# Attention scores in two halves of keys, a 352-byte pad at the upper end of SBUF, and a new work order

## The chip, the core and the metric

The kernel runs on one core of a Trainium2 chip. Its engines work side by side: TensorE (PE) multiplies matrices from SBUF into PSUM, VectorE (DVE) and ScalarE (ACT) work element by element and are the ones that read PSUM here, GpSimd (POOL) works on SBUF, and SyncE (SP) issues the DMA transfers used here. PSUM has 8 banks of 512 float32 columns on 128 partitions. The metric is the device time of one execution, in microseconds; lower is better.

## The reference

All in float32. B = 4, H = 8 heads, S = 576 positions, D = 64, so a row of the mixer has 512 channels.

```python
q_rot, k_rot = (rotate(q), rotate(k))
scores = scale * np.matmul(q_rot, k_rot.transpose(0, 1, 3, 2))
scores = scores - np.max(scores, axis=-1, keepdims=True)
attn = np.exp(scores)
attn = attn / (np.sum(attn, axis=-1, keepdims=True) + 1e-09)
x = np.matmul(attn, v)              # then the heads of a position side by side
xt = x.transpose(0, 2, 1)
h = np.maximum(xt @ w_tok1, 0.0) @ w_tok2      # 576 -> 256 -> 576
u = x + h.transpose(0, 2, 1)
h2 = np.maximum(u @ w_ch1, 0.0) @ w_ch2        # 512 -> 1536 -> 512
return u + h2
```

## The kernel before

**Stages.** First the attention, with the token mixer of batch 0 in it; then the token mixers of batches 1 to 3; then the channel mixer. Most products are made from float32r halves: each operand is split into a high and a low part, and three matmuls (high by high, high by low, low by high) add up in one PSUM bank.

**Attention.** 16 pairs of heads, one after the other in a software pipeline. For a pair, `prep` loads k, q and v, rotates k and q on GpSimd (VectorE for the first pair), transposes them on TensorE (L372) and splits them (L386 on ScalarE, L389 on VectorE). `pair` then goes through five steps, `ORDER = [0, 1, None, 2, 3]`: four row tiles of 128 queries for both heads, and `None`, the last 64 queries of both heads in one tile. Of each step:

- `qk` (L474; L444 for `None`): scores of 128 queries against 576 keys in two halves of `W2 = 288` keys, three passes each. The two heads of L474 sit in two row tiles of the array (mode "row"); L444 uses the whole array (mode "full"). Each score tile takes two neighbouring PSUM banks, one per half, asked for by `Buf(banks, True)`, so a row tile holds four banks. One PE task makes all.
- `mx` (L426, VectorE): one instruction over 128 x 576 scores in PSUM multiplies by -1/8, writes the product to `p` in SBUF and accumulates the minimum into `nm`.
- `ex` (L430, ScalarE): exponential in place in `p`, with `nm` as bias, and the sum of the row.
- `tr` (L494; L455): transposes of `p` on TensorE, two banks; `cp` (L499; L460, L464) copies them to `pt`, on ScalarE or VectorE, whichever the planner thinks will be done first.
- `pv` (L512): 20 matmuls in column tiles after steps 1 and 3 add up the output, copied to `oT` by `p1` (L515); at the end of a pair L541 transposes it and L546, L550 divide by the row sums.

**Order.** Every step is a task with an engine, an assumed duration, dependencies, buffers and a priority. `Plan.run` is a list scheduler that runs while the program is built: it takes, for each engine, the tasks that can start within `SLACK` of the earliest one, and of these the one with the lowest priority value. Priorities are 9 for a pair plus a number from the table `AT`. A change of TensorE's mode is charged `SWITCH = 0.15` us. Banks are handed out singly or as neighbouring pairs (`Banks.pick`). The token weights (`tok_weights`, `f64_split`: L581 to L602, eight instructions a block on ScalarE, VectorE and GpSimd) are tasks of the same plan with high values in `AT["tok"]`, mostly behind the attention's.

**Mixers.** The token mixer (L682, L704) and the channel mixer (L799 up, L822 down) run matmuls of 128 x 128 weights by 512 columns. The channel mixer goes through the 1536 hidden channels in four groups of 384. In each group five chunks of rows (4, 4, 4, 4 and 2 tiles of 128) pass L799 (36 matmuls a chunk, over 512 columns, 256 for the last) and L822 (9 matmuls over 512 columns a tile). L799 multiplies the weights `c1h`, `c1l` with the activations `uh`, `ul`; L822 multiplies `gh`, `gl` (the hidden layer) with the weights `c2h`, `c2l`. Weight set 0 serves groups 1 and 3, set 1 groups 2 and 4.

**Placement in SBUF.** Pools are allocated from the lower end, or, with `side="right"`, from the upper end. Set 0 and all `uh`, `ul` are in the lower pool `wc`; set 1 and all `gh`, `gl` are in the upper pool `late`, which takes the place of the token weights' upper pool `wt`. Each of these tiles has a size that is a multiple of 512 bytes a partition. In the program before, the lower ones start 128 bytes past a multiple of 512, the upper ones 480 bytes past.

Of the kernel before, what the change touches and what calls it, by code (L numbers as in the profile page):

```python
# [9 lines left out]
F32 = mybir.dt.float32  # L10
F32R = mybir.dt.float32r
U32 = mybir.dt.uint32
ACTF = mybir.ActivationFunctionType
# [175 lines left out]

AT = {'load': [372.85, 448.93, 617.75], 'rot': [1101.38, 721.17], 'pt': [672.28, 599.15], 'bd': [281.77], 'qk': [647.35, 345.47, 341.63, 278.21, 427.4], 'mx': [288.84, 281.93, 421.34, 414.86, 343.1, 594.04, 868.63, 796.12, 321.94, 410.88], 'ex': [324.09, 378.12, 428.41, 1197.56, 379.36, 390.42, 467.2, 298.25, 872.52, 998.23], 'tr': [413.54, 441.31, 579.46, 405.18, 288.79, 578.43, 339.18, 337.66, 583.08, 350.34], 'cp': [865.09, 605.58, 582.0, 378.05, 607.51, 277.93, 417.29, 455.03, 799.68, 871.15], 'pv': [796.95, 361.72], 'p1': [368.67, 355.54], 'fin': [620.48], 'tok': [1021.9, 1071.84, 1197.3, 764.64, 1275.25, 1396.39], 'inv': [427.58], 'f6': [418.08], 'tk': [1018.84, 628.55, 594.5, 1258.97]}
EARLY = 1
FIRST = -60.0
SWITCH = 0.15
SLACK = {'PE': 0.341, 'ACT': 0.121, 'DVE': 0.054, 'POOL': 0.283, 'SP': 0.289}


def act(n, sbuf=False):
# [20 lines left out]
def rope_attention_mixer_kernel(ctx: ExitStack, tc: tile.TileContext, q, k, v, w_tok1, w_tok2, w_ch1, w_ch2, tab, out):  # L220
# [37 lines left out]
    def attention(ctx):  # L258
# [3 lines left out]
        def slots(nm, n, shape, dt=F32, pool=pers, fifo=True):  # L262
            return Slots([pool.tile(shape, dt, name=f"{nm}{i}") for i in range(n)], fifo)
# [11 lines left out]
        oTs = slots("oT", 3, [P, M + P])  # L275
        ls = slots("l", 4, [P, R + 1, 2])
        ris = slots("ri", 3, [P, R + 1, 2])
        nms = slots("nm", 8, [P, 1])
        banks = Banks(psum.tile([P, 8, 512], F32, name="s"), 8)

        for r0, r1 in ((0, 2), (2, R)):
# [128 lines left out]
        def pair(n):  # L410
# [11 lines left out]
            oT = Buf(oTs)  # L422
            pv_done = []

            def mx(sb, nm, p):
                return lambda: nc.vector.tensor_scalar(out=p().rearrange("p (a b) -> p a b", a=2), in0=sb.t[:, :, 0:W2], scalar1=-D ** -0.5,  # L426
                                                       scalar2=None, op0=ALU.mult, op1=ALU.min, accum_out=nm.t)

            def ex(nm, p, l):
                return lambda: nc.scalar.activation(out=p(), in_=p(), func=ACTF.Exp, bias=nm.t, scale=-1.0, accum_out=l())  # L430

            for i, j in enumerate(ORDER):
                g = 9 * n
                at = lambda k, h=0: g + AT[k][2 * i + h]
                c = 0 if j in (0, 1) else 1
                if j is None:
                    xy = [Buf(banks), Buf(banks)]
                    sb, nm, pb = Buf(banks, True), Buf(nms), Buf(pqs)

                    def qk(sb=sb):  # L440
                        passes = [(bb.t[:, 0], kh), (bb.t[:, 1], kh), (bb.t[:, 0], kl)]
                        for c in range(2):
                            for x, (a, m) in enumerate(passes):
                                nc.tensor.matmul(sb.t[:, c, 0:W2], a, flat(m.t)[:, TL + c * W2:TL + (c + 1) * W2], start=(x == 0), stop=(x == 2))  # L444
                    x = add("PE", 0.9, qk, bdone + kd, [sb, bb, kh, kl, nm, pb], g + AT["qk"][i])
                    p = lambda pb=pb: pb.t[:, 0:S]
                    x = add("DVE", 0.68, mx(sb, nm, p), [x], [sb, nm, pb], at("mx"))
                    x = [add("ACT", 0.765, ex(nm, p, lambda: lb.t[:, R, 0:1]), [x], [nm, pb, lb], at("ex"))]
                    exps += x

                    def tr(pb=pb, xy=xy):
                        for r in range(R + 1):
                            for z in range(2):
                                c0 = r * P - (TL if z and r == R else 0)
                                nc.tensor.transpose(xy[z].t[:, r * TL:(r + 1) * TL], pb.t[halves[z], c0:c0 + P], ident[halves[z], halves[z]])  # L455

                    x = order_tr[0] = add("PE", 0.315, tr, [*x, order_tr[0]], [*xy, pb, pt[c]], at("tr"), mode="row")
                    for z in range(2):
                        def cp(e, z=z, xy=xy, c=c):
                            return lambda: e(out=pt[c].t[:, (R + 1) * z:(R + 1) * z + R, 2 * P:2 * P + TL],  # L460
                                             in_=xy[z].t[:, 0:R * TL].rearrange("p (r s) -> p r s", r=R))

                        def cpt(e, z=z, xy=xy, c=c):
                            return lambda: e(out=pt[c].t[halves[z], R, 2 * P:2 * P + TL], in_=xy[z].t[halves[z], R * TL:(R + 1) * TL])  # L464
                        two = lambda e, cp=cp, cpt=cpt: lambda: (cp(e)(), cpt(e)())
                        ev[c].append(both(two, R * TL + 2 * TL + 60, [x], [xy[z], pt[c]], at("cp")))
                    continue
                sbs, nmb, pb = [Buf(banks, True), Buf(banks, True)], [Buf(nms), Buf(nms)], Buf(ps)

                def qk(sbs=sbs, j=j):  # L470
                    for c in range(2):
                        for x, (a, m) in enumerate(((qh, kh), (qh, kl), (ql, kh))):
                            for h in range(2):
                                nc.tensor.matmul(sbs[h].t[:, c, 0:W2], flat(a.t)[halves[h], TL + j * P:TL + (j + 1) * P],  # L474
                                                 flat(m.t)[halves[h], TL * (1 - h) + c * W2:TL * (1 - h) + (c + 1) * W2], start=(x == 0), stop=(x == 2))
                t = gate[0] = add("PE", 0.9, qk, qp[0 if j < 2 else -1] + kd, [*sbs, qh, ql, kh, kl, *nmb, pb], g + AT["qk"][i], mode="row")
                xs = []
                for h in range(2):
                    p = lambda h=h, pb=pb: pb.t[:, h * S:(h + 1) * S]
                    x = add("DVE", 0.68, mx(sbs[h], nmb[h], p), [t], [sbs[h], nmb[h], pb], at("mx", h))  # L480
                    x = add("ACT", 0.765, ex(nmb[h], p, lambda h=h, j=j: lb.t[:, j, h:h + 1]), [x], [nmb[h], pb, lb], at("ex", h))
                    xs.append(x)
                exps += xs
                o = j % 2 * P

                for h in range(2):
                    xy = [Buf(banks), Buf(banks)]
                    m = R + h

                    def tr(pb=pb, xy=xy, h=h, m=m):  # L490
                        for i in range(m):
                            for z in range(2):
                                c0 = h * M + i * P
                                nc.tensor.transpose(xy[z].t[:, i * TL:(i + 1) * TL], pb.t[halves[z], c0:c0 + P], ident[halves[z], halves[z]])  # L494

                    x = order_tr[0] = add("PE", 0.06 * m + 0.015, tr, [*xs[0:h + 1], order_tr[0]], [*xy, pb, pt[c]], at("tr", h), mode="row")
                    for z in range(2):
                        def cp(e, z=z, xy=xy, c=c, o=o, h=h, m=m):
                            return lambda: e(out=pt[c].t[:, R * h:R * h + m, o + z * TL:o + (z + 1) * TL],  # L499
                                             in_=xy[z].t[:, 0:m * TL].rearrange("p (r s) -> p r s", r=m))  # L500
                        ev[c].append(both(cp, m * TL, [x], [xy[z], pt[c]], at("cp", h)))
                if j not in (1, 3):
                    continue
                w = 2 * P + (TL if c == 1 else 0)
                c0 = 2 * P * c
                ab = Buf(banks)

                def pv(c=c, w=w, ab=ab):
                    for r in range(R + 1):
                        for h in range(2):  # L510
                            m = pt[c].t[:, R if r == R else r + h * (R + 1), 0:w]
                            nc.tensor.matmul(ab.t[halves[h], 0:w], vb.t[:, h, r, :], m, start=(r == 0), stop=(r == R))  # L512

                def p1(e, w=w, ab=ab, c0=c0):
                    return lambda: e(out=oT.t[:, c0:c0 + w], in_=ab.t[:, 0:w])  # L515

                x = add("PE", 10 * (w / 1200 + 0.0025), pv, ev[c] + vdone, [ab, vb, pt[c]], g + AT["pv"][c], mode="col")
                pv_done.append(both(p1, w, [x], [ab, oT], g + AT["p1"][c]))
# [87 lines left out]
    def stage(n, src, prio, o=0, sb=None):  # L606
# [4 lines left out]
            out=sb.t[o * TL:o * TL + p, n:n + w].rearrange("p c t -> p (c t)"), in_=src.bitcast(U32)), [], [sb], prio)  # L611
        return sb, t

    wts = ctx.enter_context(ExitStack())
    wt = wts.enter_context(tc.tile_pool(name="wt", bufs=1, side="right"))
    w1h = wt.tile([P, R, FT], F32R, name="w1h")
# [298 lines left out]
```

## Time and profile before

| | before |
|---|---|
| median of 3 runs | 626.06 us (626.01 to 626.52) |
| profiled execution | 626.3 us |
| its span, first to last instruction | 624.4 us |
| TensorE busy | 600.2 us, 96% of the span |
| VectorE busy | 427.9 us, 69% |
| ScalarE busy | 316.7 us, 51% |
| GpSimd busy | 232.3 us, 37% |
| granted TensorE clock, mean | 1.000 |

The shares are means over stages that differ: VectorE and ScalarE are nearly full in the attention (0 to about 250 us) and half idle in the channel mixer (317 to 620 us), where TensorE has no gap. A busy TensorE is no proof that it is full, since matmuls overlap and one that is held up still counts; the distance between equal blocks of work tells more.

### The profile page before, as it was taken

The numbers are of one execution on the slowest core, as the hardware profiler recorded it, in microseconds if no ns is written. First come the engines' busy times: TensorE is split into PE (matmuls) and PEld (weight loads), VectorE is DVE, ScalarE is ACT, GpSimd is POOL, SyncE is SP. The second block draws the span as 40 slices with busy tenths as digits, with TensorE's granted clock in tenths as the row PEclk, the third lists the DMA queues.
The fourth block names the chain that finished last, engine by engine and source line by source line (L and its number), as shares of the span: only waits on it lengthen the run. The fifth ranks groups of instructions, "written<-read, shape, count | busy, mean of one in ns | idle before, by whom it ended". The sixth has DMA issues, their size and how long they took to land.

```text
span 624.4 us, 13199 instructions
## 1 busy us (share of the span) xinstructions
PE 600.2 (96%) x5040; PEld 475.3 (76%) x5040; DVE 427.9 (69%) x985; ACT 316.7 (51%) x811; POOL 232.3 (37%) x377
## 2 busy tenths in 40 slices
PE   3899999999999999999999999999999999999997
PEld 2777777777777777767788888888888888888886
DVE  6799999889987788479779885388334943222232
ACT  2889988999888888544335532144102411011010
POOL 3888989989888770053221020001000000000000
PEclk9999999999999999999999999999999999999999
DMA  6533223222222120003012320042001200001122
GB/s 161 155 101 97 64 62 97 71 63 64 62 64 65 42 71 3 1 26 82 13 60 66 113 75 26 1 126 77 2 0 33 70 1 0 1 0 68 68 67 101
DMA packets 33678, 36.16 MB, mean 58 GB/s; under 512 B 13776, under 2 KB 27088, under 8 KB 33616
## 3 DMA queue, kind: packets, MB, share of 16 engines
q1 hardware_dynamic: 32784, 35.01, 19.7%
q8 instruction: 39, 0.64, 0.4%
q10 hardware_dynamic: 832, 0.33, 0.2%
q14 instruction: 23, 0.19, 0.1%
HBM read 30.61 MB, written 4.72 MB: 57 GB/s over the span
## 4 chain that ended last, share of the span: by engine, by line
PE 84%; ACT 6%; DVE 5%; issue 1%; DMA 1%; POOL 1%; SPq 0%; DVEq 0%; POOLq 0%; ACTq 0%
PE m L799 24%; PE m L822 24%; PE s L512 10%; PE s L474 7%; PE s L494 5%; PE m L704 3%; PE m L682 2%; ACT p L430 2%; PE s L372 2%; DVE p L426 2%; PE s L444 2%; ACT pt L499 2%; PE s L704 1%; PE s L682 1%; PE s L541 1%
## 5 line engine op out<-in xcount | busy, mean ns | idle before, releaser
L801 ACT ACTIVATE gh<-m 128x512 fp32r<-128x512 f32 (+1 forms) x60 | 33.4, 557 | 177.3 <-PE m L799 177.1
L430 ACT ACTIVATE p<-p,nm 128x576 f32<-128x576 f32 x128 | 98.3, 772 | 12.6 <-DVE p L426 12.5
L426 DVE TENSOR_SCALAR_CACHE_REDUCE p<-s 128x576 f32<-128x576 f32 x128 | 90.7, 750 | 9.8 <-PE s L474 9.3
L799 PE MATMUL m<-uh,c1h 128*128 128x512 f32 (+1 forms) x240 | 89.1, 371 | 0.0
L799 PE MATMUL m<-uh,c1l 128*128 128x512 f32 (+1 forms) x240 | 89.0, 371 | 0.0
L799 PE MATMUL m<-ul,c1h 128*128 128x512 f32 (+1 forms) x240 | 89.0, 371 | 0.0
L803 DVE SCALAR_TENSOR_TENSOR gl<-m,gh 128x512 fp32r<-128x512 f32 (+1 forms) x60 | 38.3, 638 | 72.1 <-ACT gh L801 71.8
L824 DVE TENSOR_TENSOR X<-m,X 128x512 f32<-128x512 f32 x64 | 44.2, 691 | 59.9 <-PE m L822 59.5
L822 PE MATMUL m<-c2h,gh 128*128 128x512 f32 x216 | 85.0, 394 | 0.0
L822 PE MATMUL m<-c2h,gl 128*128 128x512 f32 x216 | 84.9, 393 | 0.0
L822 PE MATMUL m<-c2l,gh 128*128 128x512 f32 x216 | 84.9, 393 | 0.0
L512 PE MATMUL s<-pt,vraw 128*64 128x256 f32 (+1 forms) x640 | 84.4, 411 | 0.0
L593 POOL TENSOR_TENSOR fa<-fc,fa 128x384 f32<-128x384 f32 (+1 forms) x13 | 14.2, 1092 | 138.9 <-DVE fa L591 138.9
L512 PEld LDWEIGHTS s<-pt,vraw 128*64 128x64 f32 x640 | 43.2, 137 | 29.0 <-issue 1.8
L494 PEld LDWEIGHTS s<-ident,p 64*128 64x128 f32 x1152 | 45.9, 139 | 23.9 <-ACT p L430 8.7
L499 ACT COPY pt<-s 128x256 f32<-128x256 f32 (+1 forms) x170 | 57.9, 411 | 9.4 <-PE s L494 9.3
L494 PE MATMUL s<-ident,p 64*128 64x64 f32 x1152 | 54.9, 229 | 7.0 <-ACT pt L499 3.8
L474 PE MATMUL s<-kh,qh 64*128 64x288 f32 x256 | 55.2, 341 | 1.4 <-DVE p L426 0.6
L799 PEld LDWEIGHTS m<-uh,c1h 128*128 128x128 f32 x240 | 45.2, 188 | 8.5
L799 PEld LDWEIGHTS m<-ul,c1h 128*128 128x128 f32 x240 | 45.2, 188 | 8.4
L799 PEld LDWEIGHTS m<-uh,c1l 128*128 128x128 f32 x240 | 45.2, 188 | 8.1
L474 PE MATMUL s<-kl,qh 64*128 64x288 f32 x256 | 48.1, 308 | 0.0
(140 smaller groups left out, 1205.0 us busy)
## 6 DMA issues: line engine op xcount, KB each, us to landing
stg<-in_moe_w_ch_dram SPq DMA_DIRECT2D x16, 384.0 KB, 3.2
stg<-in_moe_w_ch_dram SPq DMA_DIRECT2D x12, 512.0 KB, 3.6
qraw<-in_q_dram SPq DMA_DIRECT2D x16, 256.0 KB, 2.7
vraw<-in_v_dram SPq DMA_DIRECT2D x16, 256.0 KB, 2.9
out_dram<-X SPq DMA_DIRECT2D x16, 256.0 KB, 2.3
kraw<-in_k_dram SPq DMA_DIRECT2D x15, 256.0 KB, 2.8
stg<-in_moe_w_tok_dram SPq DMA_DIRECT2D x4, 512.0 KB, 4.0
kraw<-in_k_dram SPq DMA_DIRECT2D x32, 32.0 KB, 2.6
```

The source lines that it names most:

```text
L426: return lambda: nc.vector.tensor_scalar(out=p().rearrange("p (a b) -> p a b", a=2), in0=sb.t[:, :, 0:W2], scalar1=-D ** -0.5, scalar2=Non ...
L430: return lambda: nc.scalar.activation(out=p(), in_=p(), func=ACTF.Exp, bias=nm.t, scale=-1.0, accum_out=l())
L474: nc.tensor.matmul(sbs[h].t[:, c, 0:W2], flat(a.t)[halves[h], TL + j * P:TL + (j + 1) * P], flat(m.t)[halves[h], TL * (1 - h) + c * W2:TL ...
L494: nc.tensor.transpose(xy[z].t[:, i * TL:(i + 1) * TL], pb.t[halves[z], c0:c0 + P], ident[halves[z], halves[z]])
L499: return lambda: e(out=pt[c].t[:, R * h:R * h + m, o + z * TL:o + (z + 1) * TL], in_=xy[z].t[:, 0:m * TL].rearrange("p (r s) -> p r s", r=m))
L512: nc.tensor.matmul(ab.t[halves[h], 0:w], vb.t[:, h, r, :], m, start=(r == 0), stop=(r == R))
L704: nc.tensor.matmul(tb.t[0:w], a, m, start=(i == 0), stop=(i == 5))
L799: nc.tensor.matmul(tb.t[:, 0:n], a, m, start=(i == 0), stop=(i == len(lst) - 1))
L801: x = add("ACT", act(n), lambda f=f, tb=tb: nc.scalar.activation(out=gb.t[0][:, f, 0:n], in_=tb.t[:, 0:n], func=ACTF.Relu), [x], [tb, gb], ...
L803: y = add("DVE", dve(n), lambda f=f, tb=tb: nc.vector.scalar_tensor_tensor(out=gb.t[1][:, f, 0:n], in0=tb.t[:, 0:n], scalar=0.0, in1=gb.t[ ...
L822: nc.tensor.matmul(tb.t, a, m, start=(i == 0), stop=(i == len(lst) - 1))
L824: y = add("DVE", 0.69, lambda u=u, tb=tb: nc.vector.tensor_tensor(out=u, in0=tb.t, in1=u, op=ALU.add), [z] + sums.get((ci, x), []), [tb], ...
```

## The change

- `mx` and the scores work on one half of the keys at a time. Each half is a PE task of its own (assumed 0.45 us, 0.47 for `None`, where the whole took 0.9), with single banks: two for a row tile, one for `None`. The second half's task depends on the first's.
- VectorE gets one instruction of 288 columns for each half (assumed 0.38 us, where the whole took 0.68). The first writes its minimum to column 0 of `nm`, now two columns wide; the second takes that as a second operand of the minimum and writes the result to column 1, which the exponential reads. The exponential is still one instruction over 576 columns.
- A tile of 88 float32 a partition (352 bytes) is allocated first at the upper end and never used, so that every upper tile lies 352 bytes lower.
- The table `AT` and `SLACK` have new values throughout; `AT["qk"]` has ten numbers and `AT["mx"]` twenty, one for each half.

```diff
...
-SLACK = {'PE': 0.341, 'ACT': 0.121, 'DVE': 0.054, 'POOL': 0.283, 'SP': 0.289}
+SLACK = {'PE': 0.047, 'ACT': 0.057, 'DVE': 0.089, 'POOL': 0.012, 'SP': 0.083}
...
-        nms = slots("nm", 8, [P, 1])
+        nms = slots("nm", 8, [P, 2])
...
-            def mx(sb, nm, p):
-                return lambda: nc.vector.tensor_scalar(out=p().rearrange("p (a b) -> p a b", a=2), in0=sb.t[:, :, 0:W2], scalar1=-D ** -0.5,
-                                                       scalar2=None, op0=ALU.mult, op1=ALU.min, accum_out=nm.t)
+            def mx(sb, nm, p, c):
+                return lambda: nc.vector.tensor_scalar(out=p()[:, c * W2:(c + 1) * W2], in0=sb.t[:, 0:W2], scalar1=-D ** -0.5,
+                                                       scalar2=nm.t[:, 0:1] if c else None, op0=ALU.mult, op1=ALU.min, accum_out=nm.t[:, c:c + 1])
 
             def ex(nm, p, l):
-                return lambda: nc.scalar.activation(out=p(), in_=p(), func=ACTF.Exp, bias=nm.t, scale=-1.0, accum_out=l())
+                return lambda: nc.scalar.activation(out=p(), in_=p(), func=ACTF.Exp, bias=nm.t[:, 1:2], scale=-1.0, accum_out=l())
...
-                    x = add("PE", 0.9, qk, bdone + kd, [sb, bb, kh, kl, nm, pb], g + AT["qk"][i])
                     p = lambda pb=pb: pb.t[:, 0:S]
-                    x = add("DVE", 0.68, mx(sb, nm, p), [x], [sb, nm, pb], at("mx"))
+                    x, t = None, None
+                    for u in range(2):
+                        sb = Buf(banks)
+
+                        def qk(sb=sb, u=u):
+                            for y, (a, m) in enumerate(((bb.t[:, 0], kh), (bb.t[:, 1], kh), (bb.t[:, 0], kl))):
+                                nc.tensor.matmul(sb.t[:, 0:W2], a, flat(m.t)[:, TL + u * W2:TL + (u + 1) * W2], start=(y == 0), stop=(y == 2))
+                        t = add("PE", 0.47, qk, bdone + kd + [t], [sb, bb, kh, kl, nm, pb], g + AT["qk"][2 * i + u])
+                        x = add("DVE", 0.38, mx(sb, nm, p, u), [t, x], [sb, nm, pb], g + AT["mx"][4 * i + 2 * u])
...
-                t = gate[0] = add("PE", 0.9, qk, qp[0 if j < 2 else -1] + kd, [*sbs, qh, ql, kh, kl, *nmb, pb], g + AT["qk"][i], mode="row")
+                    gate[0] = add("PE", 0.45, qk, qp[0 if j < 2 else -1] + kd + [x[0] for x in t], [*sbs, qh, ql, kh, kl, *nmb, pb], g + AT["qk"][2 * i + u], mode="row")
+                    t.append((gate[0], sbs))
                 xs = []
                 for h in range(2):
                     p = lambda h=h, pb=pb: pb.t[:, h * S:(h + 1) * S]
-                    x = add("DVE", 0.68, mx(sbs[h], nmb[h], p), [t], [sbs[h], nmb[h], pb], at("mx", h))
+                    x = None
+                    for u in range(2):
+                        x = add("DVE", 0.38, mx(t[u][1][h], nmb[h], p, u), [t[u][0], x], [t[u][1][h], nmb[h], pb], g + AT["mx"][4 * i + 2 * u + h])
...
+    ctx.enter_context(tc.tile_pool(name="edge", bufs=1, side="right")).tile([P, 88], F32, name="edge")
     wts = ctx.enter_context(ExitStack())
...
```

## Rows read from the trace of the kernel before

**Rows 1.** Busy us by stretch: engines (instructions), granted clock, DMA share, GB/s.

```profile
80.00:120.00 40.00, 37.86 (x550) 28.59 (x548) 37.88 (x102) 34.85 (x103) 36.48 (x54) 1.00 0.30 82
200.00:240.00 40.00, 39.11 (x569) 29.45 (x565) 32.56 (x96) 35.01 (x103) 28.37 (x53) 1.00 0.15 45
```

**Rows 2.** Chain that ended last, 310 us on: start us, length us, what.

```profile
310.61 6.93 PE m L704 x29
...
344.18 8.17 PE m L799 x36
352.35 16.86 PE m L822 x72
...
420.79 8.43 PE m L799 x36
429.22 8.18 PE m L822 x36
...
454.00 4.28 PE m L799 x36
```

**Rows 3.** The same chain, attention: the first value train of five pairs.

```profile
22.54 2.31 PE s L512 x20
...
56.94 2.31 PE s L512 x20
...
163.80 2.31 PE s L512 x20
...
223.16 2.36 PE s L512 x20
...
237.92 2.31 PE s L512 x20
```

**Rows 4.** The same chain, attention: stretches on VectorE, ScalarE, and one task of scores.

```profile
75.84 2.13 DVE p L426 x6
...
108.37 2.40 ACT p L430 x6
...
214.47 1.05 PE s L474 x12
```

**Rows 5.** VectorE in order of time: two minima back to back.

```profile
197.21 0.76 DVE L426 TENSOR_SCALAR_CACHE_REDUCE p<-s 128x576 f32<-128x576 f32 x1
...
197.89 0.75 DVE L426 TENSOR_SCALAR_CACHE_REDUCE p<-s 128x576 f32<-128x576 f32 x1
```

**Rows 6.** Groups by shape: one VectorE form at two widths (busy, mean ns, idle).

```profile
L803 DVE SCALAR_TENSOR_TENSOR gl<-m,gh 128x512 fp32r<-128x512 f32 x48 | 33.2, 691 | 60.1 <-ACT gh L801 59.8
...
L803 DVE SCALAR_TENSOR_TENSOR gl<-m,gh 128x256 fp32r<-128x256 f32 x12 | 5.1, 425 | 12.0 <-ACT gh L801 12.0
```

**Rows 7.** VectorE in order of time: the first rotation.

```profile
3.69 0.42 DVE L338 TENSOR_TENSOR w<-kraw,tabs 128x256 f32<-128x256 f32 x1 [3.69 <-DMA tabs<-in_tab_dram]
4.03 0.42 DVE L340 TENSOR_TENSOR uk<-kraw,tabs 128x256 f32<-128x256 f32 x1
4.49 0.29 DVE L342 TENSOR_TENSOR uk<-uk,w 128x128 f32<-128x128 f32 x1
```

**Rows 8.** The page's chain: shares of the span by line.

```profile
PE m L799 24%; PE m L822 24%; PE s L512 10%; PE s L474 7%; PE s L494 5%; PE m L704 3%; PE m L682 2%; ACT p L430 2%; PE s L372 2%; DVE p L426 2%; PE s L444 2%; ACT pt L499 2%; PE s L704 1%; PE s L682 1%; PE s L541 1%
```

**Rows 9.** Who waited for whom: us in total, times, longest us.

```profile
ACT p L430 <- DVE p L426: 12.5, 15, 1.4
...
PEld s L494 <- ACT p L430: 8.7, 16, 1.7
...
PEld s L474 <- DVE pt L499: 1.7, 6, 0.3
PEld s L474 <- DVE p L426: 1.6, 5, 0.6
```

**Rows 10.** TensorE's weight loads in order of time, into and out of L444.

```profile
213.40 0.30 PEld L444 LDWEIGHTS s<-kh,bd 128*128 128x128 f32 x2 [0.17 <-POOL uk L344]
...
214.39 0.25 PEld L474 LDWEIGHTS s<-kh,qh 64*128 64x128 f32 x2 [0.17 <-issue]
```

More of the change, by code (lines that the diff above doesn't have):

```diff
@@ L188, in run @@
         self.tasks = []
-AT = {'load': [372.85, 448.93, 617.75], 'rot': [1101.38, 721.17], 'pt': [672.28, 599.15], 'bd': [281.77], 'qk': [647.35, 345.47, 341.63, 278.21, 427.4], 'mx': [288.84, 281.93, 421.34, 414.86, 343.1, 594.04, 868.63, 796.12, 321.94, 410.88], 'ex': [324.09, 378.12, 428.41, 1197.56, 379.36, 390.42, 467.2, 298.25, 872.52, 998.23], 'tr': [413.54, 441.31, 579.46, 405.18, 288.79, 578.43, 339.18, 337.66, 583.08, 350.34], 'cp': [865.09, 605.58, 582.0, 378.05, 607.51, 277.93, 417.29, 455.03, 799.68, 871.15], 'pv': [796.95, 361.72], 'p1': [368.67, 355.54], 'fin': [620.48], 'tok': [1021.9, 1071.84, 1197.3, 764.64, 1275.25, 1396.39], 'inv': [427.58], 'f6': [418.08], 'tk': [1018.84, 628.55, 594.5, 1258.97]}
+AT = {'load': [-20.56, -15.14, 1115.59], 'rot': [413.93, -11.1], 'pt': [638.98, 626.32], 'bd': [306.27], 'qk': [342.77, 350.83, 876.15, 1225.26, 324.73, 467.22, 326.55, 279.58, 9.34, 451.2], 'mx': [-43.46, 250.81, 283.06, 300.61, 529.41, 174.25, -29.08, 519.82, 371.04, 220.05, 691.69, 279.55, 835.6, 414.22, -40.53, 344.47, 284.96, 547.85, 346.71, -20.48], 'ex': [1065.13, 201.43, 8.56, 1086.49, 1064.22, 1084.37, 307.35, 1120.75, -86.92, 682.4], 'tr': [442.05, 285.08, 291.29, 419.25, 259.2, 223.99, 15.66, 300.75, 567.21, 1101.26], 'cp': [468.17, 874.28, -11.0, -8.63, 24.13, 437.77, 296.95, 968.86, 234.41, 876.62], 'pv': [684.0, 579.56], 'p1': [1117.12, 440.26], 'fin': [1229.14], 'tok': [1034.01, 1119.51, 1228.93, 1122.5, 1530.99, 290.85], 'inv': [875.4], 'f6': [544.6], 'tk': [1026.36, 494.17, 586.69, 691.37]}
 EARLY = 1
@@ L437, in pair @@
                     xy = [Buf(banks), Buf(banks)]
[L438 to L444, printed above, removed]
-                    x = add("PE", 0.9, qk, bdone + kd, [sb, bb, kh, kl, nm, pb], g + AT["qk"][i])
-                    p = lambda pb=pb: pb.t[:, 0:S]
-                    x = add("DVE", 0.68, mx(sb, nm, p), [x], [sb, nm, pb], at("mx"))
+                    nm, pb = Buf(nms), Buf(pqs)
+                    p = lambda pb=pb: pb.t[:, 0:S]
+                    x, t = None, None
[6 more added lines that the diff above has]
+                        x = add("DVE", 0.38, mx(sb, nm, p, u), [t, x], [sb, nm, pb], g + AT["mx"][4 * i + 2 * u])
                     x = [add("ACT", 0.765, ex(nm, p, lambda: lb.t[:, R, 0:1]), [x], [nm, pb, lb], at("ex"))]
@@ L467, in pair, with qk @@
                     continue
-                sbs, nmb, pb = [Buf(banks, True), Buf(banks, True)], [Buf(nms), Buf(nms)], Buf(ps)
-                def qk(sbs=sbs, j=j):
-                    for c in range(2):
+                nmb, pb = [Buf(nms), Buf(nms)], Buf(ps)
+                t = []
+                for u in range(2):
+                    sbs = [Buf(banks), Buf(banks)]
+                    def qk(sbs=sbs, j=j, u=u):
                         for x, (a, m) in enumerate(((qh, kh), (qh, kl), (ql, kh))):
                             for h in range(2):
-                                nc.tensor.matmul(sbs[h].t[:, c, 0:W2], flat(a.t)[halves[h], TL + j * P:TL + (j + 1) * P],
-                                                 flat(m.t)[halves[h], TL * (1 - h) + c * W2:TL * (1 - h) + (c + 1) * W2], start=(x == 0), stop=(x == 2))
-                t = gate[0] = add("PE", 0.9, qk, qp[0 if j < 2 else -1] + kd, [*sbs, qh, ql, kh, kl, *nmb, pb], g + AT["qk"][i], mode="row")
+                                nc.tensor.matmul(sbs[h].t[:, 0:W2], flat(a.t)[halves[h], TL + j * P:TL + (j + 1) * P],
+                                                 flat(m.t)[halves[h], TL * (1 - h) + u * W2:TL * (1 - h) + (u + 1) * W2], start=(x == 0), stop=(x == 2))
+                    gate[0] = add("PE", 0.45, qk, qp[0 if j < 2 else -1] + kd + [x[0] for x in t], [*sbs, qh, ql, kh, kl, *nmb, pb], g + AT["qk"][2 * i + u], mode="row")
+                    t.append((gate[0], sbs))
                 xs = []
@@ L479, in pair @@
                     p = lambda h=h, pb=pb: pb.t[:, h * S:(h + 1) * S]
-                    x = add("DVE", 0.68, mx(sbs[h], nmb[h], p), [t], [sbs[h], nmb[h], pb], at("mx", h))
+                    x = None
+                    for u in range(2):
+                        x = add("DVE", 0.38, mx(t[u][1][h], nmb[h], p, u), [t[u][0], x], [t[u][1][h], nmb[h], pb], g + AT["mx"][4 * i + 2 * u + h])
                     x = add("ACT", 0.765, ex(nmb[h], p, lambda h=h, j=j: lb.t[:, j, h:h + 1]), [x], [nmb[h], pb, lb], at("ex", h))
```

## Prediction

> **What bounds the kernel now.** I read the profile in this order. First the busy time by stretch [rows 1]: between 80 and 120 us VectorE is busy 37.88 of 40 us and ScalarE 34.85; between 200 and 240 us it is 32.56 and 35.01. TensorE is busy 37.86 and 39.11, but a matmul that waits inside a train still counts as busy, so that column can't tell whether the engine is full. For that I took the chain of work that ended last, in two parts.
>
> From 310 us to the end the chain is nothing but TensorE, block after block [rows 2]. Blocks of 36 matmuls over 512 columns take either 8.17 to 8.18 us or 8.43 us (227 or 234 ns for one matmul). The reader should sort them by line and by time. The first weight group (to about 390 us) and the third (466 to 540 us) use weight set 0, the second and fourth use set 1. With set 0 the up-projection L799 is quick (344.18) and the down-projection L822 slow (352.35: 72 in 16.86 us). With set 1 it is the other way round (420.79 slow, 429.22 quick). One row of each kind stands there; the chain's other blocks of the four groups follow it. Lines and shapes are the same, so neither is the cause. What goes with it is where the operands lie: set 0 and the activations uh, ul are allocated from the lower end of SBUF, set 1 and gh, gl from the upper end. L799 with set 0 has both operands below, L822 with set 1 both above: quick. L799 with set 1 and L822 with set 0 have one operand on each side: slow.
>
> In the attention the chain shows one train of 20 value matmuls for each of 16 pairs of heads [rows 3]. From 163.80 to 237.92 us there are five pairs, 14.82 us each; from 56.94 to 163.80 seven pairs, 15.27 each; from 22.54 to 56.94 two pairs, 17.2 each. Against 14.76, the last interval, the early pairs lose 4.9 us, the middle ones 3.5, the late ones 0.3. In the middle the chain runs over VectorE (minima at 75.84, six instructions in 2.13 us) and ScalarE (exponentials at 108.37, six in 2.40) [rows 4]: where the token-weight splitting fills every gap of these two engines, TensorE is held up by them. Later there is room.
>
> **The pad.** It adds no instruction. It moves every upper tile 352 bytes down. From the allocation of the kernel before, lower tiles of the mixers start 128 bytes past a multiple of 512, upper ones 480 past; 480 - 352 = 128, so both sides then agree. My reading of [rows 2] is that a matmul is slow when its two operands lie differently against such a boundary. The slow matmuls are L799 in groups 2 and 4 (2 x 4 full chunks x 36 = 288) and L822 in groups 1 and 3 (2 x (4 x 36 + 18) = 324), together 612, or 17 blocks of 36. Each would save 8.43 - 8.18 = 0.25 us: 4.25 us, all on the chain. The last chunk's blocks of 36 matmuls over 256 columns take 4.28 us with set 1 (454.00) and no less with set 0, so they don't show it, and I count nothing there. Ends: 0 and -4.25. I take -4.25, since the four combinations sort without exception.
>
> [...]
>
> **Scores and minima in halves.** Matmuls are the same in number and shape. VectorE gets two instructions of 288 columns for one of 576, 9 scores x 16 pairs = 144 times. Back to back, the 576-column form starts every 0.68 us (197.21, 197.89), though it lasts 0.76 [rows 5]. The width costs (691 - 425)/256 = 1.04 ns a column by another VectorE form that reads PSUM [rows 6], so 288 columns fewer save 0.30 us and a half costs 0.38: two cost 0.76, 0.08 more. That is 144 x 0.08 = 11.5 us of VectorE, 0.72 a pair. The second half reads the first one's minimum. Where they stand next to each other VectorE must wait for it: the rotation at the start shows an independent instruction (4.03) starting 0.34 us after one that lasts 0.42, and a dependent one (4.49) 0.46 after [rows 7], so 0.12 us. Ends for that: none, if the other head's half stands between (in the four row-tiled tasks it can), and 9 a pair, 1.1 us. Queued behind such a wait are the copies pt and the other minima, for which the transposes and exponentials wait.
>
> [...]
>
> How much of the 11.5 us is on the path? The minima have 2% of the chain, 12.5 us [rows 8], or 18 scores at 0.68. 18 x 0.08 = +1.5 us (with the dependency wait each time, +3.7). The rest lies under TensorE's 14.76 us a pair: without weight splitting VectorE is busy 32.56/40 x 14.76 = 12.0 us a pair [rows 1], 12.7 after, at worst 13.8. It takes room from the weight splitting, though, which must last longer. That fills the 2.7 us a pair that were free; 11.5 us would be four pairs more, but the copies that may run on either engine can take half of it to ScalarE. Two more pairs at the middle loss of 0.5 us (3.5 over seven): +1.0 (ends 0 and +2).
>
> **What it gives.** With L474 at 1.05 us for a task [rows 4], the two heads' minima are ready 1.73 and 2.41 us after its start (1.05 + 0.68, + 0.68). In halves the first pair of banks is ready at 0.53, and four halves of 0.38 end at 0.91, 1.29, 1.67 and 2.05. The first exponential can start 0.06 earlier and the second 0.36, 0.21 on average. ScalarE waits for a minimum 15 times, 12.5 us, and the transposes' weight loads for an exponential 16 times, 8.7 us [rows 9]. 15 x 0.21 = 3.2 us; I take two thirds, -2.0, as 8.7 is to 12.5 (ends 0 and 16 x 0.36 = -5.8). A task no longer needs two neighbouring banks for each head before it starts. Weight loads of L474 wait 1.7 us for a copy that leaves a bank and 1.6 us for a minimum [rows 9], 3.3 us in all; I take half, -1.6 (ends 0 and -3.3), for what comes late next is the copy itself.
>
> **Changes of tiling mode.** The shared-tail scores L444 use the whole array, between row-tiled tasks. Going in leaves 0.17 us of weight-load idle (213.40), coming out 0.17 (214.39) [rows 10]. Should the two halves be parted by a row-tiled task, a pair pays 0.34 twice: +0.34 x 16 = 5.4 us. I take 0: after the first half the planner's own switching charge of 0.15 is above the new TensorE slack of 0.047, so the second half is preferred if its bank is free. Ends 0 and +5.4.
>
> **The new queue and slacks.** They alter nothing that is computed, only the order. Loads go earlier for k and q and later for v on SP; the DMA engines are busy 30% of the time in the middle and 15% later [rows 1], so I price that at nothing. No row prices a new order. Its bounds are the pairs' losses above: -8.7 if no pair lost anything, and as much again in the other direction. I take 0.
>
> **Sum.** -4.25 + 1.5 + 1.0 - 2.0 - 1.6 = -5.35 us. The profiled execution took 626.3 us (span 624.4 and 1.9 around it), 0.2 above the median of 626.06. From the median: 620.7.
>
> **Rivals.** (a) The pad does nothing; the attention alone gives -1.1: 625.0. [...] Against it: no other property sorts the four. (b) VectorE becomes the bound of the attention, slower than before. Price: 0.72 us a pair on the path for all 16, +11.5, less 4.25: 633.3. It decides where VectorE's work passes the pair's time: at 80 to 120 us it has 37.88 of 40 us, and 2.7 pairs x 0.72 = 1.9 make 39.8, full; with dependency waits it is over. Against it: the weight splitting there is no part of a pair and can move to 200 us and later. (c) The finer tasks and the new order take out nearly all losses of early and middle pairs, 8.4 us, with the pad's 4.25 beside them: 613.4. For it: single banks give the planner more places. Against it: the stretches at 75.84 and 108.37 are full engines, not missing banks. (d) The tail's halves are parted: -5.35 + 5.4, or 626.1.
>
> **How the numbers follow.** This kernel's time can be told from no change from about 0.2% on, 1.25 us. Forecast 0.52 (faster but for 0.02), (c) 0.20, (a) 0.12 (half faster, 0.05 same, 0.01 slower), (d) 0.07 (0.05 same, 0.02 slower), (b) 0.09. Faster 0.76, same 0.12, slower 0.12. The range leaves out (b), and of (c) the half below 614.5, and takes in (a) and most of (d): 614.5 to 626.1.
>
> **What would show it.** The pad: no L799 or L822 block of 36 above 8.25 us, and the stretch from the first L799 to the end about 4 us shorter. The halves: L426 288 times, about 0.38 us apart, VectorE 11 to 25 us busier, fewer holes in front of L474. The queue: value trains 14.7 to 15.0 us apart from the fifth pair on, weight splitting until 180 to 200 us. Wrong it would be if slow blocks remain, if VectorE trains stand in front of the exponentials throughout, or if L444's two halves stand apart.

## The result and the profile after

The changed kernel takes 619.3 us (median of 4 runs, 618.73 to 619.74) where the kernel before took 626.29 beside it: ratio 0.9876, 95% interval 0.9852 to 0.9899. That is 7.0 us less; 5.35 were forecast. The profiled execution has a span of 617.4 us, 7.0 below the 624.4 of before.

Line numbers move by the change: scores L477 and L446 (were L474, L444), transposes L500 (L494), copies L505 (L499), value train L518 (L512), up- and down-projection L806 and L829 (L799, L822). L426 and L430 are as before.

First the chain of work that ended last, from the channel mixer on (start us, length us, what). These lines answer to [rows 2].

```profile
315.45 16.32 PE m L806 x72
...
333.43 8.39 PE m L829 x36
341.81 8.16 PE m L806 x36
349.98 16.32 PE m L829 x72
...
416.92 8.16 PE m L806 x36
425.08 8.16 PE m L829 x36
...
449.56 4.31 PE m L806 x36
...
613.58 0.69 DVE X L831
```

The blocks of 36 over 512 columns now take 8.16 us with either weight set, on either line, and 8.19 us behind a last chunk. One stands out, 8.39 us at 333.43, behind other matmuls (L780): it took 8.63 at 335.55 before, so it lost as much as the other slow blocks and still lies above the 8.25 us that the prediction allowed. The stretch from the first L806 to the last addition is 298.13 us; before it was 302.98 (317.54 to 620.52). So 4.85 us of the 7.0 come from here, and 2.1 from everything that lies ahead.

The attention looks different from what was expected. Page: busy time, VectorE by slice, and the chain's shares; then the stretches of [rows 1].

```profile
PE 593.7 (96%) x5040; PEld 472.4 (77%) x5040; DVE 448.3 (73%) x1291; ACT 310.8 (50%) x786; POOL 236.8 (38%) x384
DVE  6899999999999999779769895399334943323232
PE 68%; DVE 23%; ACT 5%; issue 3%; DMA 1%; ACTq 0%; DVEq 0%
PE m L806 24%; PE m L829 24%; DVE p L426 13%; PE s L518 4%; PE s L500 3%; ACT p L430 3%; PE s L477 2%; PE m L711 2%; DVE pq L426 2%; PE s L372 2%; PE m L689 1%; PE s L711 1%; PE s L689 1%; PE s L456 1%; DVE kl L389 1%
```

```profile
80.00:120.00 40.00, 38.20 (x574) 29.31 (x574) 38.67 (x138) 36.32 (x106) 35.42 (x59) 1.00 0.26 72
...
200.00:240.00 40.00, 39.54 (x582) 30.14 (x579) 38.67 (x148) 34.36 (x101) 28.58 (x51) 1.00 0.13 38
```

VectorE is full from the first pairs to the last (38.67 of 40 us in both stretches; before 37.88 and 32.56, [rows 1]). What fills it is the pairs' own work and no longer the splitting of token weights: VectorE spends some 8 us on that (lines L587 to L608) up to 240 us, where it had spent 25 by 177 us before. Its minima have 15% of the chain (13 for `p`, 2 for `pq`) where they had 2 [rows 8]. Yet a pair takes less time: the first value train of a pair stands at 160.67, 175.52 and 190.09 us in the chain, 14.6 to 14.9 apart. In TensorE's order of time, which the experiments below go by, the late pairs are 14.56 us apart.

```profile
160.67 2.31 PE s L518 x20
...
175.52 2.31 PE s L518 x20
...
190.09 2.31 PE s L518 x20
...
234.50 2.31 PE s L518 x20
```

```profile
190.02 2.38 PE L518 MATMUL s<-pt,vraw 128*64 128x256 f32 x20
...
204.58 2.38 PE L518 MATMUL s<-pt,vraw 128*64 128x256 f32 x20
```

By the sixteenth pair (234.50, before 237.92 in [rows 3]) the attention is 3.4 us ahead, and 3.3 at its end (260.81, before 264.10). Of this 1.2 us are lost again in the token mixers: from 274 to 295 us the chain runs over VectorE, which splits weights there beside their work, where before it was back on TensorE at 281.67. No run isolates this loss.

VectorE in order of time shows why it is so full. Columns as in [rows 5]: start, length, line, operation, tiles.

```profile
197.36 0.45 DVE L426 TENSOR_SCALAR_CACHE_REDUCE p<-s 128x288 f32<-128x288 f32 x1
...
197.73 0.45 DVE L426 TENSOR_SCALAR_CACHE_REDUCE p<-s 128x288 f32<-128x288 f32 x1
...
198.32 0.52 DVE L426 TENSOR_SCALAR_CACHE_REDUCE p<-s,nm 128x288 f32<-128x288 f32 x1
...
198.76 0.45 DVE L426 TENSOR_SCALAR_CACHE_REDUCE p<-s 128x288 f32<-128x288 f32 x1
```

A first half takes 0.37 to 0.38 us from start to start (197.36, 197.73), as worked out. A second half, which reads `nm`, takes 0.44 (198.32, 198.76). And the second half at 198.32 starts 0.59 us after the first half in front of it, 0.21 more than that one needs: it waits for a minimum just made. Between 160 and 235 us such waits of 0.11 to 0.21 us come three times a pair, about 0.45 us together. So a pair pays 9 x 0.08 + 9 x 0.06 + 0.45 = 1.7 us of VectorE, where 0.72 were counted. The groups by shape agree (515 against 453 ns):

```profile
L426 DVE TENSOR_SCALAR_CACHE_REDUCE p<-s,nm 128x288 f32<-128x288 f32 x128 | 64.2, 515 | 3.9 <-PE s L477 0.4
L426 DVE TENSOR_SCALAR_CACHE_REDUCE p<-s 128x288 f32<-128x288 f32 x128 | 55.5, 453 | 1.0 <-PE s L477 0.9
```

### The profile page after: what moved, and what is told of

It is laid out like the page before. It is cut to its first block, busy times and chain, and to the rows that moved or that the text cites. A ratio compares the mean times of both kernels' runs of the same rounds, so it can differ in the third digit from the quotient of the medians.

```text
span 617.4 us, 13456 instructions
## 1 busy us (share of the span) xinstructions
PE 593.7 (96%) x5040; PEld 472.4 (77%) x5040; DVE 448.3 (73%) x1291; ACT 310.8 (50%) x786; POOL 236.8 (38%) x384
## 4 chain that ended last, share of the span: by engine, by line
PE 68%; DVE 23%; ACT 5%; issue 3%; DMA 1%; ACTq 0%; DVEq 0%
PE m L806 24%; PE m L829 24%; DVE p L426 13%; PE s L518 4%; PE s L500 3%; ACT p L430 3%; PE s L477 2%; PE m L711 2%; DVE pq L426 2%; PE s L372 2%; PE m L689 1%; PE s L711 1%; PE s L689 1%; PE s L456 1%; DVE kl L389 1%
## 5 line engine op out<-in xcount | busy, mean ns | idle before, releaser
L430 ACT ACTIVATE p<-p,nm 128x576 f32<-128x576 f32 x128 | 99.7, 780 | 27.4 <-DVE p L426 24.9
L806 PE MATMUL m<-uh,c1h 128*128 128x512 f32 (+1 forms) x240 | 88.4, 368 | 0.0
L806 PE MATMUL m<-uh,c1l 128*128 128x512 f32 (+1 forms) x240 | 88.3, 368 | 0.0
L806 PE MATMUL m<-ul,c1h 128*128 128x512 f32 (+1 forms) x240 | 88.3, 368 | 0.0
L518 PE MATMUL s<-pt,vraw 128*64 128x256 f32 (+1 forms) x640 | 84.4, 411 | 0.0
L829 PE MATMUL m<-c2h,gh 128*128 128x512 f32 x216 | 84.2, 390 | 0.0
L829 PE MATMUL m<-c2l,gh 128*128 128x512 f32 x216 | 84.1, 389 | 0.0
L829 PE MATMUL m<-c2h,gl 128*128 128x512 f32 x216 | 84.0, 389 | 0.0
L426 DVE TENSOR_SCALAR_CACHE_REDUCE p<-s,nm 128x288 f32<-128x288 f32 x128 | 64.2, 515 | 3.9 <-PE s L477 0.4
L518 PEld LDWEIGHTS s<-pt,vraw 128*64 128x64 f32 x640 | 43.2, 137 | 29.2 <-DVE p L426 2.6
L599 POOL TENSOR_TENSOR fa<-fc,fa 128x384 f32<-128x384 f32 (+2 forms) x14 | 16.2, 1158 | 128.4 <-DVE fa L597 125.6
L500 PEld LDWEIGHTS s<-ident,p 64*128 64x128 f32 x1152 | 42.1, 141 | 19.7 <-issue 11.6
L426 DVE TENSOR_SCALAR_CACHE_REDUCE p<-s 128x288 f32<-128x288 f32 x128 | 55.5, 453 | 1.0 <-PE s L477 0.9
L500 PE MATMUL s<-ident,p 64*128 64x64 f32 x1152 | 49.4, 229 | 4.7 <-ACT p L430 3.1
L505 ACT COPY pt<-s 128x256 f32<-128x256 f32 (+1 forms) x159 | 52.1, 402 | 0.6 <-PE s L500 0.6
L806 PEld LDWEIGHTS m<-uh,c1h 128*128 128x128 f32 x240 | 45.2, 189 | 7.7
L806 PEld LDWEIGHTS m<-ul,c1h 128*128 128x128 f32 x240 | 45.2, 189 | 7.6
L806 PEld LDWEIGHTS m<-uh,c1l 128*128 128x128 f32 x240 | 45.2, 189 | 7.5
L477 PE MATMUL s<-kh,qh 64*128 64x288 f32 x256 | 49.5, 347 | 1.2 <-ACT qh L386 0.5
```

Of the source, the lines that this page charges most:

```text
L426: return lambda: nc.vector.tensor_scalar(out=p()[:, c * W2:(c + 1) * W2], in0=sb.t[:, 0:W2], scalar1=-D ** -0.5, scalar2=nm.t[:, 0:1] if c ...
L477: nc.tensor.matmul(sbs[h].t[:, 0:W2], flat(a.t)[halves[h], TL + j * P:TL + (j + 1) * P], flat(m.t)[halves[h], TL * (1 - h) + u * W2:TL * ( ...
L806: nc.tensor.matmul(tb.t[:, 0:n], a, m, start=(i == 0), stop=(i == len(lst) - 1))
L829: nc.tensor.matmul(tb.t, a, m, start=(i == 0), stop=(i == len(lst) - 1))
```

## Experiments on the pad

The theory: a matmul of the channel mixer is slow when its two operands lie differently against some boundary, and the pad makes them agree. The rival: the quick blocks have another cause.

**The pad alone.** The kernel before with the one line:

```diff
+    ctx.enter_context(tc.tile_pool(name="edge", bufs=1, side="right")).tile([P, 88], F32, name="edge")
     wts = ctx.enter_context(ExitStack())
```

> The kernel before with the 352-byte pad alone. Theory (a matmul is slow when its two operands lie differently against a boundary): every block of 36 matmuls over 512 columns takes 8.16 us, the channel mixer is 4.3 to 4.9 us shorter, the attention is as before: 621.4 to 622.0 us. Rival (the quicker blocks after the change have another cause, such as other work beside them): slow blocks stay, 626.3 us.

Measured: 621.72 us, ratio 0.9899 (0.9861 to 0.9937). The blocks take what they take in the changed kernel (here down-projection with set 0, up-projection with set 1, the two that were slow), and the attention's trains stand within 0.5 us of where they stood.

```profile
352.30 16.32 PE m L823 x72
...
419.23 8.16 PE m L800 x36
```

**The change without the pad.** The same line taken out of the changed kernel.

> The changed kernel without the pad. Theory: the slow blocks at 8.43 us return with set 1 in L799's place and with set 0 in L822's, 619.3 + 4.85 = 624.2 us. Rival: 619.3 us, all blocks quick.

Measured: 624.13 us, ratio 0.9945 (0.9923 to 0.9968), with 8.43 to 8.44 us on L806 (named L805 there) with set 1 and on the down-projection (L828) with set 0:

```profile
350.07 16.87 PE m L828 x72
...
418.52 8.43 PE m L805 x36
```

The rival falls: the pad is worth 4.9 us (626.6 - 621.7) in the old kernel and 4.8 (624.1 - 619.3) in the new one.

**Which boundary.** Two pads of other sizes in the changed kernel:

```diff
-.tile([P, 88], F32, name="edge")
+.tile([P, 8], F32, name="edge")      # second run: [P, 24]
```

> The changed kernel with a pad of 32 bytes in place of 352: upper tiles 448 bytes past a multiple of 512, lower ones 128, difference 320 = 5 x 64. If only the place within 64 bytes counts: all blocks 8.16 us, about 619.3 us. If the place within 128 bytes or more counts: slow blocks as without a pad, about 624.

> The same with a pad of 96 bytes: upper tiles 384 past, difference 256. If the place within 64, 128 or 256 bytes counts: all blocks quick, 619.3 us. If it is within 512: slow, about 624.

Measured: 624.52 us with 32 bytes, 618.92 with 96, one execution each. The chain of the first, in the order set 0 (two lines), set 1 (two lines):

```profile
342.88 8.19 PE m L806 x36
351.06 16.80 PE m L829 x72
...
402.73 8.40 PE m L806 x36
411.13 8.18 PE m L829 x36
```

A difference of 320 bytes is slow (8.40), one of 256 is quick (8.16, as with the full pad). Without a pad it was 352: slow. So agreeing within 64 bytes is not enough, and agreeing within 512 is not needed. The place within 128 bytes or within 256 fits all four; a difference of 128 was not run, so which of the two is open. What in the chip makes such a matmul 3% longer no run shows. The token mixer's train at 310.61 us of [rows 2] (both operands above; 29 matmuls in 6.77 us from start to start, 233 ns on average) is no counterexample: its matmuls start 226 to 227 ns apart in its middle, as in a quick block; the average is raised by the first, 341 ns, and by some of 229 to 240 near both ends.

## Experiments on the halves and the order

**Order and halves apart.** The new order on whole scores, and the old order on halves:

```diff
 # halves, old order (pad kept): changed kernel
-AT = {...}; SLACK = {'PE': 0.047, ...}
+AT = {... of before, each half with the whole's number ...}; SLACK = {'PE': 0.341, ...}
 # whole scores, new order: kernel before with the pad
-AT = {...}; SLACK = {'PE': 0.341, ...}
+AT = {... of the changed kernel, the whole with its second half's number ...}; SLACK = {'PE': 0.047, ...}
```

> Halves and pad with the old order: table and slacks of the kernel before, each half with the whole's priority. If the halves themselves make the attention shorter (single banks, earlier exponentials): about 2 us under the pad alone, 619 to 620. If the new order is what does it, the halves alone only load VectorE (144 x 0.14 = 20 us more): 622 to 630.

> Whole scores in pairs of banks as before, with the pad and the new order (table and slacks of the changed kernel, the whole with its second half's priority). If the order does it without the halves: 619 to 620. If the halves are needed: at or above the pad alone, 621.5 to 626.

Measured: halves with the old order 635.44 us, ratio 1.0121 (1.0078 to 1.0164); whole scores with the new order 659.58, ratio 1.0491 (1.0447 to 1.0535). Against 621.72 for the old order with whole scores and the pad, the halves alone lose 13.7 us and the order alone 37.9; together they win 2.4. Both lie beyond what was expected if the other part were needed (630 and 626), and neither is a gain by itself. But each run has an order that was made for the other kind of score tasks, and an order for ten of them has no exact counterpart for five; the second run's mean granted clock is also 0.966, and how much of its loss goes with that was not separated. The two numbers show that halves and order belong together; they don't price either.

**The second half's operand taken away.** Order and dependencies of the plan stay; only the instruction changes, so that its shift leaves out the first half:

```diff
-scalar2=nm.t[:, 0:1] if c else None
+scalar2=None
```

> The changed kernel, but the second half's minimum doesn't take the first half's as an operand, so the exponential is shifted by the minimum of the second half alone (the row sums divide it out). The planner's order is kept. It takes 0.06 us and a possible wait from 144 VectorE instructions. If VectorE, full at 38.7 of 40 us, sets the attention's time: 5 to 10 us less, 609 to 614 us. If weight splitting only fills what is free and the pairs are bound elsewhere: within 1.5 us of 619.3.

Measured: 607.03 us, ratio 0.9681 (0.9656 to 0.9705), 12.3 us under the changed kernel and below the 609 to 614 expected. Back to back, all halves now start 0.38 us apart. VectorE does bound the changed kernel's attention. With that taken off, the chain leaves VectorE (stretch as in [rows 1]; the page's chain by engine; value trains in TensorE's order of time):

```profile
160.00:200.00 40.00, 40.00 (x605) 30.62 (x602) 38.31 (x158) 36.00 (x107) 36.08 (x62) 1.00 0.27 70
```

```profile
PE 90%; DVE 4%; ACT 2%; issue 1%; DMA 1%; ACTq 0%; POOL 0%; DVEq 0%; POOLq 0%
```

```profile
181.27 2.38 PE L518 MATMUL s<-pt,vraw 128*64 128x256 f32 x20
...
195.12 2.38 PE L518 MATMUL s<-pt,vraw 128*64 128x256 f32 x20
```

TensorE is busy 40.00 of 40 us and the chain has no other engine in it from 160 to 198 us. VectorE is still busy 38.31 of 40 us, so its busy share would not have told that it no longer sets the time. A pair takes 13.86 us (mean of the three pairs from 167.41 to 208.98 us). The matmuls are the same in number and shape, so the 14.76 of before was not TensorE's own need.

**Operand without the wait.** The second half reads a constant column in place of the first half's minimum (again a shift that leaves out the first half):

```diff
-scalar2=nm.t[:, 0:1] if c else None
+scalar2=ident[:, 0:1] if c else None
```

> The changed kernel, the second half's minimum taking a constant column (0 or 1 in a partition) as its second operand in place of the first half's minimum, so the shift leaves out the first half. The instruction with a second operand stays (0.44 us apart instead of 0.38, 9 x 0.06 = 0.54 us a pair), the wait for the first half goes (0.11 to 0.21 us, three times a pair in the trace, 0.44 a pair). If VectorE's occupancy is what counts, the time lies between 607.0 without both and 619.3 with both, near 612.5. If the operand's price is everything: 619; if the wait is everything: 607.

Measured: 611.38 us, ratio 0.9745 (0.9717 to 0.9772), near the 612.5 expected, and no waits between halves any more: a second half right behind a first one starts 0.38 us after it. The page's chain by engine:

```profile
PE 88%; DVE 7%; ACT 2%; issue 1%; DMA 1%; ACTq 0%; POOL 0%; DVEq 0%; POOLq 0%
```

Taken off in this order, the wait is worth 7.9 us (619.3 - 611.4), the dearer instruction 4.3 (611.4 - 607.0). A pair takes 14.10 us:

```profile
183.28 2.38 PE L518 MATMUL s<-pt,vraw 128*64 128x256 f32 x20
...
197.38 2.38 PE L518 MATMUL s<-pt,vraw 128*64 128x256 f32 x20
```

**The dear form in both halves.** The first half reads the constant column too, and the second the running minimum as in the changed kernel:

```diff
-scalar2=nm.t[:, 0:1] if c else None
+scalar2=nm.t[:, 0:1] if c else ident[:, 0:1]
```

> The changed kernel, the first half's minimum taking the same constant column as a second operand, so that all 288 halves have the dear form: 9 x 0.06 = 0.54 us of VectorE a pair more, order unchanged. If VectorE sets the attention's time: 16 x 0.54 = 8.6 us more, 626 to 628. If it is full only of filling work: 619 to 620.5.

Measured: 628.11 us, ratio 1.001 (0.9993 to 1.0026), 8.8 us above the changed kernel, with pairs 15.08 us apart (mean of the three from 180.48 to 225.73 us):

```profile
180.48 2.38 PE L518 MATMUL s<-pt,vraw 128*64 128x256 f32 x20
...
195.57 2.38 PE L518 MATMUL s<-pt,vraw 128*64 128x256 f32 x20
```

Against the changed kernel's 14.56, VectorE's time passes to the pair one for one: +0.54 us of VectorE a pair gave +0.52, -0.45 gave -0.46. The last step, -0.54, gave less (-0.24). By then the chain is already TensorE's: in the run with the constant column VectorE has 7% of it, in the changed kernel 23%. That this run still gained 0.24 us a pair from cheaper VectorE work shows that a chain on TensorE alone, too, can hold time that another engine costs. So 13.86 us is a bound from above of what TensorE needs for a pair.

**The halves' price without the halves' use.** The old kernel with the pad, whole scores and old order, but the minimum in two instructions:

```diff
-nc.vector.tensor_scalar(out=p()..., in0=sb.t[:, :, 0:W2], ..., scalar2=None, ..., accum_out=nm.t)
+for c in range(2):
+    nc.vector.tensor_scalar(out=p()[:, c * W2:(c + 1) * W2], in0=sb.t[:, c, 0:W2], ..., scalar2=nm.t[:, 0:1] if c else None, ..., accum_out=nm.t[:, c:c + 1])
```

> The kernel before with the pad, whole scores in pairs of banks, old order; only the minimum is taken in two VectorE instructions, the second with the first one's result as operand and right behind it. VectorE gets 0.08 + 0.06 + 0.11 to 0.21 = 0.25 to 0.35 us a score, 2.3 to 3.2 us a pair, and nothing of what the halves give. If the halves' cost is on the path: 12.0 us of VectorE a pair become 14.3 to 15.2, more than the weight splitting leaves room for, 635 to 650 us. If TensorE hides it: 621.7 to 624.

Measured: 654.36 us, ratio 1.0426 (1.0398 to 1.0455): 32.6 us above the pad alone, and above the 635 to 650 expected. The stretch from 80 us on:

```profile
80.00:120.00 40.00, 35.02 (x446) 25.77 (x446) 37.33 (x122) 30.32 (x82) 27.79 (x44) 0.93 0.23 62
```

VectorE holds the attention up, TensorE is idle for 5 of 40 us, and the granted TensorE clock is 0.93 there, where the kernel before has 1.00 [rows 1]. How much of the 32.6 us goes with this lower clock was not separated, so the price can't be read off exactly. That the dearer minima are on the path without the smaller tasks is clear: they have 14% of the chain, where they had 2.

**Another way to the full minimum.** Both halves plain, and the smaller of the two found on GpSimd:

```diff
-scalar2=nm.t[:, 0:1] if c else None
+scalar2=None
...
+if c:
+    nc.gpsimd.tensor_scalar(out=nm.t[:, 1:2], in0=nm.t[:, 1:2], scalar1=nm.t[:, 0:1], scalar2=None, op0=ALU.min)
```

> The changed kernel with both halves' minima taken alone on VectorE and the smaller of the two found by a GpSimd instruction on one column, issued behind the second half, so that the full minimum is used. VectorE's occupancy is that of the run without the operand. If that alone counts: 607 to 609. If the handover VectorE to GpSimd to ScalarE, some 0.3 to 0.5 us before each exponential, is on the path: 610 to 616. If GpSimd, busy 36 to 38 of 40 us, has no room for 144 more: up to 622.

Measured: 660.69 us, ratio 1.0526 (1.0498 to 1.0554), above all three guesses. Who waited for whom (us, times, longest):

```profile
ACT p L434 <- POOL nm L430: 52.3, 64, 3.4
POOL nm L430 <- DVE p L427: 27.7, 28, 3.6
```

The exponentials wait 52.3 us for GpSimd, up to 3.4 us at once (and the mean granted clock is 0.974): the small instruction, itself 0.28 us long (median of 81 between 80 and 240 us), stands in line behind rotations, and the rotations behind its own wait for VectorE. In front of the longest wait GpSimd works on rotations and casts from 80.78 us on and reaches the minimum at 85.52. The planner knew nothing of the 144 instructions, so an order made with them stays untried. The free engine was not free, and a queue that waits passes its waits on.

**The planner told the right price.**

```diff
-x = add("DVE", 0.38, mx(...), ...)
+x = add("DVE", 0.45 if u else 0.38, mx(...), ...)
```

> The changed kernel, with the planner told 0.45 us for a second half (0.44 is its measured distance) where it assumed 0.38. Nothing else differs but the order that follows. If the order loses time because the planner thinks VectorE freer than it is: 1 to 3 us less, as more copies go to ScalarE. If the order was found for the wrong price and fits only that: 1 to 5 us more.

Measured: 670.08 us, ratio 1.0702 (1.0673 to 1.0731). The second guess was right in its sign and far too small. The mean granted clock was 0.964, and the slices of the page show it low in places, all ahead of the channel mixer (which starts at 363.9 us, in the 22nd slice):

```profile
PEclk9889998977989999989899999999999999999999
```

A change of 0.07 us in an assumed duration reorders the queue: the first value trains of the pairs from 101 to 267 us now stand 12 to 24 us apart, and 51 us are lost. The order holds for this program with its assumed numbers. How much of the 51 us is the clock and how much the order was not separated.

## Why the prediction came out

The time lay in the range, 1.4 us below the forecast. The pad's part was understood; that the attention's part came out near its number is luck. Step by step:

- **What bounds the channel mixer, and the pad.** The reading of [rows 2] was right. 4.25 us were forecast and 4.85 came: the 17 slow blocks gave 0.27 us each instead of 0.25, about 4.55 together, and about 0.3 came from the blocks that were called quick, which went from 8.17 to 8.21 to 8.16 or 8.19. The rival that the pad does nothing fell with the runs with the pad alone and without it.
- **VectorE's price.** The term of 0.08 us a score for the width was right (0.38 us a half). The step that failed is the list of what a second half costs: the operand's own 0.06 us had no term, and the wait, allowed for between 0 and 1.1 us a pair, was about 0.45 and was taken as nothing. 1.7 us a pair instead of 0.72.
- **How much of it is on the path.** +1.5 us were set from the minima's 2% of the old chain; afterwards they have 15%, and the operand and the wait alone cost 12.3 us. The step that failed is that VectorE's 12.7 us a pair, at worst 13.8, would lie under TensorE's 14.76. Worked out in the same way VectorE is busy 38.67/40 x 14.56 = 14.1 us a pair, and with 0.45 us of waits that is the whole pair. The minima alone explain 1.3 of the 2.1 us more; the rest is other work, among it one of a pair's two copies to `oT` (0.35 us), of which ScalarE had made both in the late pairs. The prediction's own sign of being wrong was there: VectorE's minima stand in front of the exponentials in the chain from the first pairs to the last. The rival "VectorE becomes the bound" had the mechanism right. Its time, 633.3 us, was wrong because it added the price to pairs of 14.76 us.
- **What the halves give.** -3.6 us were forecast for earlier exponentials and single banks. With the operand and the wait taken away, halves in their own order are 14.7 us shorter than whole scores in theirs, both with the pad (621.7 - 607.0). The failing step is the use of 14.76 us as what TensorE needs for a pair; 13.86 are enough. Counted from each matmul's start to the next, the row-tiled scores of a late pair took 4.12 us before (pair from 208.31 us) and take 3.66 in the run without the operand (from 195.12), the transposes 2.81 and 2.41: nearly all of the 0.9 us. How much of this is single banks, how much earlier exponentials and how much the order, no run separates.
- **The two together.** -14.7 and +12.3 give the attention's -2.4, where -3.6 and +2.5 were forecast. Two large terms, both mis-sized, nearly cancelled.
- **The order.** Priced at nothing with bounds of 8.7 us to either side. Between halves with the old order and with the new one lie 16 us (635.4 and 619.3), so the bounds were too narrow. No row of before could have given it.
- **Mode changes.** Right: in none of the changed kernel's 16 pairs does another matmul stand between the two halves of L446, so the 5.4 us of parted halves did not come.
- **Weight splitting.** It was expected to last until 180 to 200 us; the last token weights were split at 260.7 us, when the attention ended.

The fastest run, 607.03 us, is below both kernels. It shifts each row by the maximum of its last 288 keys alone, which the row sum divides out as long as no score of the first half lies so far above that the exponential overflows. No run here finds the full maximum at that time.

## What to carry to other kernels

When an instruction is split in two, price the second one by its own form: what the link between the two costs (an operand more, a wait for a result just made) can be as much as the split itself, and should be tried alone, with the order of everything else held. The interval of an engine that looks full is not its need as long as waits inside its trains count as busy, and a chain that stays on that engine is no proof either; taking work off another engine and looking whether the interval falls is. And look at equal blocks of work of unequal length before anything else: here 352 unused bytes were worth more than a new attention schedule.

## What the runs showed of the hardware

- In the channel mixer 36 matmuls of 128 x 128 weights by 512 columns took 8.40 to 8.44 us (233 to 234 ns each) with operands that lie 320 or 352 bytes apart modulo 512, and 8.16 to 8.21 us (227 to 228 ns) at 0 and 256. The block behind other matmuls (L780) took 8.63 us at 352 and 8.39 at 0.
- A VectorE minimum over 128 x 288 of PSUM takes 0.38 us from start to start, and 0.44 with a column as second operand, be it the first half's minimum or a constant. Behind a minimum just made, a wait of 0.11 to 0.21 us came on top; with the constant column none did.
- In the run with the minimum in two instructions the granted clock was 0.93 between 80 and 120 us, with TensorE busy 35.02 of 40 us. With the dear form in both halves, where VectorE's time passed to the pair one for one, it was 1.00, with TensorE busy 36.53 of 40. What lowers the clock no run shows.
